# Whole weights in place of two halves for the products beside attention's queries

## The chip, the cores and the metric

The kernel runs on one core of a Trainium2 chip. The metric is the device time of one execution in microseconds (us). TensorE multiplies (PE in the profile; PEld are its weight loads), VectorE (DVE), ScalarE (ACT) and GpSimd (POOL) work on elements, SyncE (SP) issues nearly all transfers.

## The reference

Attention without a softmax, a norm over each head, and a feed-forward block behind it. The feed-forward weights arrive as 64-bit floats.

```python
kv = np.einsum('bhsd,bhse->bhde', k, v)          # 8 batches, 8 heads, 576 tokens, 64 wide
out = np.einsum('bhsd,bhde->bhse', q, kv)
rms = np.sqrt(np.mean(out * out, axis=-1, keepdims=True) + 1e-06)
x = (out / rms * g_norm)                         # -> (4608, 512)
h = x @ w_in                                     # (512, 2048)
r = np.maximum(h, 0.0)
return ((r * r) @ w_out)                         # (2048, 512)
```

## The kernel before

**Tiling.** The 4608 tokens are nine strips of 512 (`N_STRIP`), and each strip is four tiles of 128 tokens. The feed-forward block of a strip has an up part (x times w_in, squared ReLU) and a down part (times w_out). Both use Strassen's scheme: a block product is computed as seven smaller ones of sums and differences of the blocks, in the order of `ORDER` or `DEEP_ORDER`. In strip 0 the up part is plain (`up_first`, L898), and its down part has one level. Strip 1 has one level in the up part (`up`) and two in the down part (`down_deep`). From strip 2 on (`DEEP_UP`) both parts have two levels: seven products of seven small products each.

**Small products.** A small product of the up part is `up_small`: four 128 by 128 products, each with 128 rows of contraction, 128 columns of weights and 128 columns of moving activations. In the down part it is `small_products`: four products that add up in one 128 by 128 place of PSUM. Both call `halved_product` for each of the four. It issues two matmuls with 64 columns of weights each, the second writing the other 64 partitions of PSUM (L852). The one-level products go through `product` (L857), with 128 columns of weights and 256 of moving data. Everything is in 32-bit floats.

**Attention.** It runs beside the feed-forward work, a strip or more ahead, as a list of small steps, `slices`. The ones that use PE late in the kernel are `key_value` (L435: k times v, 128 rows by 64 columns of weights, then the rest of the tokens with 64 rows by 64 columns) and `products_x` (L471: the queries times kv, 64 rows by 64 columns, 64 matmuls for a pair of tiles, 32 for a single one). The step `query` calls `key_value` first if it was given keys, then `products_x`, then squares on ACT. The further steps (means, roots, scaling, a transpose, sending x to DRAM) are on DVE, ACT and SP.

**What sets the order.** The program order of each engine is that in which Python issues: there is no scheduler behind it. From strip 2 on the loop at the end of the kernel has 55 slots for the up part (`up_slot`) and 14 steps for the down part. After each slot, `attend_between` looks at the next slices and issues them when its estimates of the backlog of DVE and ACT allow it (`ON_DVE`, `ON_ACT`, `BEHIND`). So a run of queries comes at the end of a slot, between the small products of two slots. The planner's estimates do not depend on how a small product is issued. In strip 1, slices are spread evenly over the first 25 steps by `attend`.

**Tiles that products wait for.** PSUM has five buffers for products (`ps_A`, `ps_B`, `ps_C` take turns) and one each for x_ps (two banks) and other uses. A buffer comes free when ACT or DVE has read it (`snap`, L1315, is such a copy).

Of the kernel before, what the change touches and what calls it, by code (L numbers as in the profile page):

```python
# [20 lines left out]
def kernel(  # L21
# [34 lines left out]
    nc = tc.nc  # L56
# [17 lines left out]
    DEEP_UP = 2  # L74
# [216 lines left out]
    def minus(eng, out, a, b):  # L291
        eng.tensor_tensor(out=out, in0=a, in1=b, op=ALU.subtract)  # L292
# [125 lines left out]
    def key_value(b, *ps_of):  # L418
        while any(f == load and a[:2] == (b, p) or f == load_rest and a[0] == b for _, f, a in keys_due for p in ps_of):
            _, f, a = keys_due.popleft()  # L420
            f(*a)
        ps = apsum.tile([P, len(ps_of), D], FP32, name="kv_ps", tag="at")
        if (b, ps_of[0]) == (0, 0):
            keep_busy(ps[:, 0], 3)
            warm = apsum.tile([P, NT, P], FP32, name="x_ps", tag="first")[:, 0]
        half = slice(REST * (b % 2), REST * (b % 2 + 1))
        tiles = [[main.pop((n, b, p)) for n in "kv"] for p in ps_of]
        steps = [(i, c) for i in range(len(ps_of)) for c in range(C)] + [(i, C) for i in range(len(ps_of))]
        for i, c in steps:
            if (b, ps_of[i], c) == (0, 0, C):  # L430
                keep_busy(warm, 2)
            for h in range(2):
                at = (slice(None), h, c) if c < C else (half, 2 * ps_of[i] + h)
                a, w = (t[at] for t in (tiles[i] if c < C else (k_rest, v_rest)))
                nc.tensor.matmul(  # L435
                    ps[ts(h, D), i], lhsT=a, rhs=w, start=i == 0 and c == 0, stop=c == C, skip_group_check=True
                )
        at = (NP * b + ps_of[0]) % (2 * NP)
        d = kv_all[:, at : at + len(ps_of)]
        nc.scalar.copy(d[0:D, :, 0:D], ps[0:D])  # L440
        nc.scalar.copy(d[D:P, :, D:P], ps[D:P])
        for i, p in enumerate(ps_of):
            kvd[b, p] = d[:, i]
            if b < 2:
                if b == 1 and p == 0:
                    load_next()
            else:
                u = next(to_load, None)
                if u is not None:
                    keys_later(load, *u, nc.sync, "kv")  # L450
                if p == (1 if b > 3 else NP - 1) and b + 1 < B:
                    keys_later(load_rest, b + 1, nc.sync)
# [3 lines left out]
    def products_x(ns):  # L456

        ps = apsum.tile([P, 2, 2, d_model // 2], FP32, name="x_ps", tag="x", bufs=1)
        for p in range(NP):
            for i, n in enumerate(ns):  # L460
                m, c = divmod(n, PAIR)
                for h in range(2):
                    half = slice(REST * h, REST * (h + 1))
                    if c == C:
                        q, b = qT["rest", m, p], 2 * m + h
                    else:
                        b, c_b = (2 * m, c) if c < C else (2 * m + 1, c - C - 1)
                        q = qT[b, p][:, c_b]
                    for r in range(2):
                        row = slice(D * r, D * (r + 1))  # L470
                        nc.tensor.matmul(  # L471
                            ps[half, r, i, ts(p, D)], lhsT=q[row, half], rhs=kvd[b, p][row, row], start=True, stop=True
                        )
        return ps

    def squared_parts(parts, pool=xn_pool, tag="x_n"):
        sqs = []
        for ps in parts:
            sqs.append(pool.tile(list(ps.shape), FP32, name="sq", tag=tag))
            nc.scalar.activation(sqs[-1], ps, AF.Square)  # L480
        return sqs
# [26 lines left out]
    def query(ns, *keys):  # L508
        if keys:
            key_value(*keys)  # L510
        ps = products_x(ns)
        parts = [ps[:, :, i] for i in range(len(ns))]
        queried.append((parts, squared_parts(parts, c_pool, "c")))

    def query_means(ns):
        ps = products_x(ns)
        parts = [ps[:, :, i] for i in range(len(ns))]
        queried.append((parts, mean_of(squared_parts(parts))))
# [171 lines left out]
    slices, ready = [], {}  # L690
# [30 lines left out]
    for b in range(2, B):  # L721
        pairs = query_pairs(b)
        for i, pair in enumerate(pairs):
# [8 lines left out]
            if more and b > 2 and left == 1 + b % 2:  # L732
                slices.append((T, (b + 1, 0)))
            slices.append((query, (pair, *keys)))
            if b == 2:
                slices += [(T, (3, 1))] * (left == 1) + [(mean_roots, (pair,)), (normalized, (pair,))]
# [20 lines left out]
    slice_at = [0]  # L757
# [84 lines left out]
    def open_bank(p):  # L842
# [2 lines left out]
            bank[b] = fpsum.tile([P, 2, 2 * P], FP32, name=f"ps_{b}", tag="f")  # L845
        return bank[b]

    def halved_product(ps, lhsT, rhs, start, stop):

        for h in range(2):  # L850
            half = slice(P // 2 * h, P // 2 * (h + 1))
            nc.tensor.matmul(ps[half], lhsT=lhsT[:, half], rhs=rhs, start=start, stop=stop, skip_group_check=True)  # L852
# [21 lines left out]
    def quarters(s, g):  # L874

        if (s, 11) not in gq:
            for q in (11, 12, 21, 22):
                gq[s, q] = g_pool.tile([P, FQ, TH], FP32, name="gt", tag="gt")
        return {q: gq[s, q][:, 2 * g : 2 * g + 2, :] for q in (11, 12, 21, 22)}
# [6 lines left out]
    def sum_g3(s, g):  # L886
        dest = quarters(s, g)
        minus(nc.vector, dest[12], dest[11], dest[12])
# [182 lines left out]
    def small_products(s, p, js):  # L1071
        c = "B" if p in (4, 2, 5, 3) else "A"
        if js[0] == 1 and p not in (6, 7, 3):
            opened[c] = set()
            n = 2 + (s == N_STRIP - 1 and p == 5)
            chain[c] = [fpsum.tile([P, 4, P], FP32, name=f"ps_{c}", tag="f") for _ in range(n)]
            if n == 3:
                chain[c].append(apsum.tile([P, 2, 4, P], FP32, name="ps_x", tag="x", bufs=1)[:, 0])
                chain[c].append(apsum.tile([P, 4, P], FP32, name="ps_at", tag="at"))
        for j in js:  # L1080
            x, i = place(s, p)[j]
            a, w = leaf[p][j], w_blk.pop((s, p, j))
            for f in range(FQ // 2):
                halved_product(
                    chain[c][x][:, i, :], a[:, f, :], w[:, f, :], x not in opened[c] and f == 0, f == FQ // 2 - 1
                )
            opened[c].add(x)
# [199 lines left out]
    def up_small(s, n, p, j, slot):  # L1287
# [6 lines left out]
        for i in range(4):  # L1294
            if j in (5, 6, 3):
                w = w_blk["in", s, p][:, (5, 6, 3).index(j), ts(i, P)]
            else:
                kc, f = {1: (0, 0), 2: (1, 0), 4: (1, 1), 7: (0, 1)}[j]
                w = w_half(b, kc, f)[:, i // 2, ts(i % 2, P)]
            halved_product(ps[:, i, :], w, rhs, j in (1, 2, 5) and i == 0, True)  # L1300
# [47 lines left out]
    for s in range(N_STRIP):  # L1348
# [13 lines left out]
        n_up = len(steps)  # L1362
# [5 lines left out]
        goal, begun = ready.get(s + 1, len(slices)), slice_at[0]  # L1368
        if s >= DEEP_UP:
            goal = max(goal, min(ready[DEEP_UP] + (len(slices) - ready[DEEP_UP]) * (s - 1) // (N_STRIP - DEEP_UP - 1), len(slices)))  # L1370
            if s > DEEP_UP:
                goal = min(pair_ends, key=lambda end: abs(end - goal))
        total, done = sum(w for w, _, _ in steps), 0
        for i, (w, fn, a) in enumerate(steps):
# [25 lines left out]
            if s == 0 and n_up + 2 <= i < n_up + 4:  # L1400
                for g in range(2 * (i - n_up) - 4, 2 * (i - n_up) - 2):
                    sum_g3(0, g)
            fn(*a)
            if s == 0 and i < 4:

# [91 lines left out]
```

## Time and profile before

| what | value |
|---|---|
| median of three runs | 874.2 us |
| the three runs | 869.32, 874.2, 876.95 us |
| time of the profiled execution | 869.32 us |
| its span, first to last instruction | 867.5 us |
| granted TensorE clock | 1.0 over the whole span |
| matmuls | 14176, and as many weight loads |
| halved matmuls in strips 1 to 8 (L852) | first at 195.5 us, mean of one 273 ns |
| weight load of a half / of a whole L857 product | 137 / 190 ns |
| runs of query products (L471) behind 195.5 us | 13, from 244.3 to 706.3 us |
| runs of key-value products (L435) behind 195.5 us | 9 |

How to read it: a matmul's duration reaches from the start of its pass to the last result in PSUM, and several are under way at a time. What one costs in a stream is therefore the distance from its start to the next one's, which the timeline gives as the start of a group and the number of matmuls in it, and the single records give one by one. In the timeline each line is a group of like instructions: start, time from the first one's start to the last one's end, engine, line, operation, result<-operands, rows*columns of the weights, shape of the moving data, count. The page names the waits that the profile infers from semaphores. A stretch in which PE is between two shapes of matmul has no such row.

### The profile page before, as it was taken

Reading aid. Unit: us, or ns where it says so; the run is one execution under the profiler, and the core shown is the slowest. Engines: PE = TensorE matmul, PEld = TensorE weight load, DVE = VectorE, ACT = ScalarE, POOL = GpSimd, SP = SyncE. Lnnn points to the kernel's source line nnn. Section 1 sums busy time; section 2 is a strip of 40 time slices with the busy share of each in tenths; the row PEclk is TensorE's granted clock in tenths of the full one; section 3 lists DMA queues with packets and bytes.
Section 4 is the critical chain, followed back from the end, with each engine's and each line's share of the span. In section 5 each row is a group of like instructions: output and inputs, shape, how many; then the busy total and the mean of one; then the engine's idle time right before and its main releaser. Section 6 shows DMA issues by size and latency. Waiting matters only on the chain.

```text
span 867.5 us, 32585 instructions
## 1 busy us (share of the span) xinstructions
PE 860.8 (99%) x14176; PEld 805.7 (93%) x14176; DVE 720.3 (83%) x1236; ACT 352.2 (41%) x805; POOL 315.2 (36%) x319
## 2 busy tenths in 40 slices
PE   9999999999999999999999999999999999999998
PEld 7445888889999999999999999999999999999998
DVE  3999998879877996789689977897889777976887
ACT  5799251320048403750356034901491148102810
POOL 1100004630459323730574045704470447145700
PEclk9999999999999999999999999999999999999999
DMA  9998997999999997989688979997668856875483
GB/s 317 302 339 251 279 376 229 285 325 374 290 256 262 343 319 230 238 311 335 211 244 272 341 240 265 287 311 268 210 223 301 303 168 215 294 283 195 173 313 126
DMA packets 169470, 236.47 MB, mean 273 GB/s; under 512 B 78704, under 2 KB 133744, under 8 KB 161008
## 3 DMA queue, kind: packets, MB, share of 16 engines
q1 hardware_dynamic: 169024, 234.33, 83.5%
q8 instruction: 111, 1.82, 0.9%
q14 instruction: 31, 0.25, 0.1%
q10 hardware_dynamic: 304, 0.07, 0.0%
HBM read 197.66 MB, written 36.70 MB: 270 GB/s over the span
## 4 chain that ended last, share of the span: by engine, by line
PE 83%; DVE 9%; ACT 3%; DMA 3%; issue 2%; SPq 0%; DVEq 0%; ACTq 0%
PE ps_A L852 36%; PE ps_B L852 32%; PE ps_C L852 5%; PE ps_A L857 4%; PE kv_ps L435 2%; DVE w_c L272 2%; PE x_ps L471 2%; PE ps_B L857 2%; DVE w_t L292 1%; DMA w_deep<-w_t 1%; DVE wt L292 1%; DMA first_qkv<-in_v_dram 1%; DVE w_c L266 1%; PE ps_C L857 1%; DVE w_in L275 1%
## 5 line engine op out<-in xcount | busy, mean ns | idle before, releaser
L852 PE MATMUL ps_B<-w_blk,g_s 128*64 128x128 f32 x2016 | 121.8, 273 | 0.0
L852 PEld LDWEIGHTS ps_B<-w_blk,g_s 128*64 128x64 f32 x2016 | 112.4, 137 | 0.1
L852 PE MATMUL ps_A<-x_l,w_in 128*64 128x128 f32 x1568 | 102.8, 273 | 0.7 <-ACT snap L1315 0.6
L292 POOL TENSOR_TENSOR x_l<-xT 128x256 f32<-128x256 f32 x21 | 16.1, 765 | 228.6 <-PE ps_A L852 228.6
L852 PE MATMUL ps_B<-w_blk,gt 128*64 128x128 f32 x1504 | 93.9, 273 | 0.0
L852 PE MATMUL ps_A<-w_blk,g_s 128*64 128x128 f32 x1536 | 92.0, 273 | 0.0
L852 PEld LDWEIGHTS ps_A<-x_l,w_in 128*64 128x64 f32 x1568 | 89.0, 137 | 0.9 <-ACT snap L1315 0.8
L1310 POOL TENSOR_TENSOR snap<-snap,gt 128x512 f32<-128x512 f32 x35 | 46.3, 1322 | 113.4 <-ACT snap L1315 104.1
L852 PEld LDWEIGHTS ps_A<-w_blk,g_s 128*64 128x64 f32 x1536 | 85.5, 137 | 0.0
L852 PEld LDWEIGHTS ps_B<-w_blk,gt 128*64 128x64 f32 x1504 | 84.4, 137 | 0.3 <-issue 0.3
L1315 ACT COPY snap<-ps_A 128x512 f32<-128x512 f32 x63 | 36.9, 585 | 103.6 <-PE ps_A L852 94.4
L1250 ACT ACTIVATE gt<-gt 128x512 f32<-128x512 f32 x112 | 70.1, 626 | 8.8 <-DVE gt L1310 8.8
L1251 ACT ACTIVATE gt<-gt 128x512 f32<-128x512 f32 x112 | 70.7, 631 | 3.6
L852 PE MATMUL ps_A<-w_blk,gt 128*64 128x128 f32 x1152 | 71.0, 273 | 0.0
L1099 ACT COPY o_sb<-ps_A 128x128 f32<-128x128 f32 x24 | 6.4, 266 | 144.9 <-PE ps_A L852 115.4
L852 PEld LDWEIGHTS ps_A<-w_blk,gt 128*64 128x64 f32 x1152 | 64.5, 137 | 0.0
L292 DVE TENSOR_TENSOR gt<-gt 128x2048 f32<-128x2048 f32 (+1 forms) x29 | 59.7, 2063 | 0.0
L1098 DVE TENSOR_TENSOR o_sb<-o_sb,ps_B 128x256 f32<-128x256 f32 (+1 forms) x123 | 47.5, 386 | 14.5 <-ACT o_sb L1099 9.4
L1310 POOL TENSOR_TENSOR gt<-gt,snap 128x512 f32<-128x512 f32 x42 | 52.6, 1282 | 14.9 <-DVE snap L1310 14.9
L852 PE MATMUL ps_B<-x_l,w_blk 128*64 128x128 f32 x784 | 51.4, 273 | 0.0
L852 PE MATMUL ps_A<-x_l,w_blk 128*64 128x128 f32 x784 | 51.2, 273 | 0.0
L1099 ACT COPY o_sb<-ps_B 128x128 f32<-128x128 f32 x31 | 8.2, 266 | 96.3 <-PE ps_B L852 96.3
(194 smaller groups left out, 1838.1 us busy)
## 6 DMA issues: line engine op xcount, KB each, us to landing
w_blk<-w_deep SPq DMA_DIRECT2D x56, 1024.0 KB, 7.2
w_blk<-w_out SPq DMA_DIRECT2D x56, 768.0 KB, 6.5
w_blk<-w_in_deep SPq DMA_DIRECT2D x49, 768.0 KB, 6.0
raw<-in_moe_w_in_dram SPq DMA_DIRECT2D x16, 512.0 KB, 7.8
raw<-in_moe_w_out_dram SPq DMA_DIRECT2D x16, 512.0 KB, 5.2
k<-in_k_dram SPq DMA_DIRECT2D x29, 256.0 KB, 5.1
v<-in_v_dram SPq DMA_DIRECT2D x29, 256.0 KB, 5.3
x_d<-x_q SPq DMA_DIRECT2D x27, 256.0 KB, 4.9
```

Source lines behind the costliest of these rows:

```text
L272: yield nc.vector.scalar_tensor_tensor(out=ci, in0=high, scalar=-(2**30), in1=ci, op0=ALU.bitwise_and, op1=ALU.bitwise_or)
L292: eng.tensor_tensor(out=out, in0=a, in1=b, op=ALU.subtract)
L435: nc.tensor.matmul(ps[ts(h, D), i], lhsT=a, rhs=w, start=i == 0 and c == 0, stop=c == C, skip_group_check=True)
L471: nc.tensor.matmul(ps[half, r, i, ts(p, D)], lhsT=q[row, half], rhs=kvd[b, p][row, row], start=True, stop=True)
L852: nc.tensor.matmul(ps[half], lhsT=lhsT[:, half], rhs=rhs, start=start, stop=stop, skip_group_check=True)
L857: nc.tensor.matmul(bank[BANK[p]][:, i, :], lhsT=lhsT(k), rhs=rhs(k), start=p in (1, 5, 2) and i == 0 and k == 0, stop=k == n - 1, skip_gro ...
L1098: add = lambda out, a, b: nc.vector.tensor_tensor(out=out, in0=a, in1=b, op=ALU.add)
L1099: yield nc.scalar.copy(q[:, 3:4], small(1))
L1250: nc.scalar.activation(o, o, AF.Relu)
L1251: nc.scalar.activation(o, o, AF.Square)
L1310: add = lambda eng, out, a, b: eng.tensor_tensor(out=out, in0=a, in1=b, op=ALU.add)
L1315: nc.scalar.copy(t, ps)
```

## The change

A counter, `whole`, is added. While it is positive, `halved_product` issues one matmul with all 128 columns of weights and counts down; at zero it issues two halves as before. `query` sets the counter to 12 when its products are issued, which is three small products. The loop sets it to at least 4, one small product, ahead of a step of the up part from strip 2 on, when the next slice is a query. Where the planner holds a query back for some slots, that happens at each of them.

```diff
@@ query
         parts = [ps[:, :, i] for i in range(len(ns))]
         queried.append((parts, squared_parts(parts, c_pool, "c")))
+        whole[0] = BEHIND_QUERY
@@ halved_product
+    AHEAD, BEHIND_QUERY = 4, 12
+    whole = [0]
+
     def halved_product(ps, lhsT, rhs, start, stop):

+        if whole[0]:
+            whole[0] -= 1
+            nc.tensor.matmul(ps, lhsT=lhsT, rhs=rhs, start=start, stop=stop, skip_group_check=True)
+            return
         for h in range(2):
             half = slice(P // 2 * h, P // 2 * (h + 1))
             nc.tensor.matmul(ps[half], lhsT=lhsT[:, half], rhs=rhs, start=start, stop=stop, skip_group_check=True)
@@ the loop over the steps of a strip
+            if DEEP_UP <= s and i < n_up and slice_at[0] < goal and slices[slice_at[0]][0] == query:
+                whole[0] = max(whole[0], AHEAD)
             fn(*a)
```

As built, this gives 264 whole products: 12 at the start of the down part of strip 1, where the last queries of strip 1's up part had set the counter, 12 behind each of 13 runs of queries, and 96 in groups of 4 to 16 in front of 12 of these runs.

## The prediction

> **What bounds the kernel now.** I read the page's busy shares first, then the chain that ended last, then the waits of PE, and last the timeline of PE around one visit of attention's queries. The page:
>
> ```profile
> PE 860.8 (99%) x14176; PEld 805.7 (93%) x14176; DVE 720.3 (83%) x1236; ACT 352.2 (41%) x805; POOL 315.2 (36%) x319
> ...
> PE 83%; DVE 9%; ACT 3%; DMA 3%; issue 2%; SPq 0%; DVEq 0%; ACTq 0%
> PE ps_A L852 36%; PE ps_B L852 32%; PE ps_C L852 5%; PE ps_A L857 4%; PE kv_ps L435 2%; DVE w_c L272 2%; PE x_ps L471 2%; PE ps_B L857 2%; DVE w_t L292 1%; DMA w_deep<-w_t 1%; DVE wt L292 1%; DMA first_qkv<-in_v_dram 1%; DVE w_c L266 1%; PE ps_C L857 1%; DVE w_in L275 1%
> ```
>
> PE is busy 99% of the span, and the halved products (L852) alone are 73% of the chain. The DVE and DMA shares of the chain lie before 195 us, ahead of every edit. The waits of PE from 190 us to the end are two short rows:
>
> ```profile
> PE ps_A L852 <- ACT snap L1315: 0.6, 1, 0.6
> PE x_ps L471 <- issue: 0.2, 1, 0.2
> ```
>
> So behind 195 us the end is the sum of PE's start-to-start times, and whatever is added between two matmuls there is added to the kernel. I therefore work in start-to-start times, not in durations: a half lasts 273 ns, but 112 of them take 6.11 us in the chain, that is 109.1 ns per pair of halves.
>
> **What a change of shape costs.** PE runs three shapes here: halves (128 rows by 64 columns of weights, L852; the key-value products L435 have the same shape), the queries' 64 by 64 (L471), and whole ones (128 by 128). One visit of queries between halves, timeline of PE (start, us from first start to last end, then the group):
>
> ```profile
> 438.71 1.04 PE L852 MATMUL ps_A<-x_l,w_in 128*64 128x128 f32 x16
> 439.69 0.34 PE L471 MATMUL x_ps<-kv_all,qT_rest 64*64 64x64 f32 x8
> 439.85 0.30 PE L471 MATMUL x_ps<-kv_all,qT 64*64 64x64 f32 x8
> 439.97 0.30 PE L471 MATMUL x_ps<-kv_all,qT_rest 64*64 64x64 f32 x8
> ...
> 440.55 0.30 PE L471 MATMUL x_ps<-kv_all,qT 64*64 64x64 f32 x8
> 440.78 1.09 PE L852 MATMUL ps_C<-x_t,w_in 128*64 128x128 f32 x16
> 441.70 0.50 PE L852 MATMUL ps_B<-x_t,w_blk 128*64 128x128 f32 x6
> ```
>
> Sixteen halves take 0.873 us in a steady run. Before the queries they take 0.98: leaving halves costs 0.10. Behind the queries they take 0.92: entering halves costs 0.05 (the single records say 160 ns from the first pair to the second, against 109). Entering the queries costs 0.05 too (0.16 to the second group, against 0.117), and leaving them 0.11; both stay. A change of shape is thus about 0.15 us in which PE multiplies nothing.
>
> The whole shape at 128 columns of moving data stands in the opening, where first_queries (L585) comes behind halves, and where transposes (L611) go over to halves (L407):
>
> ```profile
> 9.22 1.09 PE L407 MATMUL t_ps<-ident,q 128*64 128x128 f32 x16
> 10.24 1.16 PE L585 MATMUL x_ps<-kv_all,qT 128*128 128x128 f32 x8
> 11.33 0.69 PE L435 MATMUL kv_ps<-v,k 128*64 128x64 f32 x16
> ```
>
> ```profile
> 15.20 0.66 PE L611 MATMUL xt_ps<-ident,x_n 128*128 128x128 f32 x4
> 15.78 1.09 PE L407 MATMUL t_ps<-ident,first_qkv 128*64 128x128 f32 x16
> ```
>
> The sixteen halves of L407 take 1.02 us: 0.873, plus 0.05 for entering and 0.10 for leaving. The eight whole ones of L585 start 213 ns apart once and then 112, 112, 111 (single records): a steady whole product costs 111.7 ns, and entering whole costs 0.102. That a first load of 128 columns isn't hidden shows also in L857, whose first matmul behind the queries at 109.43 us is followed after 320 ns, the others after 216. Leaving whole for L435 or L407 costs 0.093 (205 against 112; 203 against 109), and 0.05 for entering the halves.
>
> So the steady rates hardly differ, 111.7 against 109.1, and **the price is in the changes of shape**. For this last point a rule of the Trainium skill says otherwise: by "TensorE: Matmul & The Clock Gate", Part 3 (Packing small matmuls), a weight load runs beside matmuls in flight only where the row group differs. L585 uses all rows in each product and still starts every 112 ns, so this trace disagrees; by that rule each whole product would take the 213 ns of an unhidden load and the change would cost 27 us.
>
> **The change part by part.** The order of instructions of the two built programs is the same on every engine but PE, DMA queues included; no wait is added and nothing is moved past anything. On PE 264 pairs of halves become 264 whole products, from 195 us on. What follows from where they stand:
>
> 1. The first 12 follow the last L857 products, which are whole already. Before: whole to halves; after: the same change 12 products later. Nothing.
> 2. Thirteen visits of queries have 12 whole products behind. Entering whole in place of halves: 13 x (0.102 - 0.051) = 0.66 us.
> 3. Behind these 12 there is a change from whole to halves that did not exist: 13 x (0.093 + 0.051) = 1.87 us.
> 4. Eleven of the visits get a group of 4 to 16 whole ones in front, behind halves: 11 x (0.100 + 0.102) = 2.22 us. Of the other two, one gets none (the call of the planner takes the slice of means and the query in one step), and one has 8 between keys and queries, where it enters whole in place of halves: 0.05 us.
> 5. In seven of the eleven, key-value products stand between the group and the queries. They have the shape of halves, and before there was no change (L852 to L435 goes on at the steady distance, 102 to 103 ns from a second half to the next first). After: 7 x (0.093 + 0.049) = 0.99 us. In the other four the whole group is left for the queries in place of halves: 0.093 against 0.100, nothing.
> 6. 264 x (111.7 - 109.1) ns = 0.69 us.
>
> The sum is 0.66 + 1.87 + 2.22 + 0.05 + 0.99 + 0.69 = **6.5 us**, all on PE and all behind 195 us, so nothing hides it. What can be taken off: one stall of PE in the records, at 551.43 us, 0.76 us over the steady distance (the first row of PE's waits gives 0.6 of it to ACT's snap), lies 15 us behind a visit. A later PE waits less there. How much cannot be read, since most of the delay in front of the queries delays ACT's work on them as much; only the 0.2 us behind the queries is a true head start for ACT. I take 0.1 and keep 0 and 0.76 as ends. In the other direction, a group delayed by some tenths of a microsecond could find ACT or POOL in a new place; the largest such stall in the trace is that same 0.76, so I allow one of them.
>
> Against the profiled execution (869.3 us, span 867.5): 869.3 + 6.4 = 875.7. The three runs before spread from 869.32 to 876.95 around the median 874.2, so the profiled one is the fastest of them; on the median the forecast is **880.6 us**, slower by 0.7%. The ends of the costs: 6 could be nothing (109.1 for the whole too, as the transposes of L611 have it), and the stall gone whole: 6.5 - 0.69 - 0.76 = 5.0. Upward: 6.5 + 0.76 = 7.3. So 879.2 to 881.5 from the terms, to which the spread of the runs adds some 3 us on both sides.
>
> **Rivals.**
>
> *The whole shape needs no emptying of PE.* If PE pulled the load of a whole product ahead across the border, terms 2 to 5 would vanish, and the way out of the queries (0.11 + 0.05) with them: 0.69 - 13 x 0.16 - 0.76 = -2.2 us, 872.0, no slower than before. It decides at the first matmul behind the queries. For it: only that L641 and L857, both whole, follow each other with no loss. Against it: L857 behind L471 at 109.43 us starts 0.148 behind the last query product, just as L852 does, and then loses 0.104 more. I find no way to a gain over 1%; that would need 8.7 us, and all thirteen visits with everything lost around them (0.10 + 0.05 + 0.11 + 0.05 each) hold 4.0.
>
> *Whole products run at the unhidden load.* If operands of the small products (strided parts of the activations, weights just fetched) kept the load from running ahead, each would cost up to 213 ns as the first of L585 does: 264 x (213 - 109) = 27.5 us in place of term 6, with 5.8 of the changes: 33 us, 907, slower by 3.8%. Any mean above 121 ns for the whole ones would carry the sum past 1%. For it: no whole product at this size with these operands is in the trace. Against it: L585 at 112, and L857 at 216 for twice the columns, with weights from gt and w_blk.
>
> *The stalls multiply.* Each visit puts 0.4 to 0.55 us into PE's order; the planner spaces ACT's work behind queries by its own costs. If each visit met one new stall like that at 551 us: 13 x 0.76 = 9.9 us on top, 890. Against it: a later PE gives the engines that feed it time, it doesn't take any.
>
> **How the numbers follow.** Forecast, slower by 5.0 to 7.3 us: 0.84. Free changes of shape: 0.06. Unhidden loads or stalls: 0.10. With a median of runs that spread by 7.6 us, a measurement tells about 1% from no change, and the forecast lies just inside: from 880.6 to the bound at 882.9 are 2.3 us, which the spread of a median (some 3 us, an estimate from the range of the three runs) and of the terms goes past about one time in five. So slower by over 1%: 0.84 x 0.21 + 0.10 = 0.28. Faster by over 1%: 0.02, from the spread in the first rival. Within 1%: 0.70. The range is 875 to 887: the terms with the spread of medians on both sides, with a little toward the stalls, and leaves out the ends of the rivals.
>
> **What the changed profile should show.** Whole products at 128 x 128 in groups of 4 to 16, 264 in all and 264 matmuls fewer; the first of each group lasting some 0.10 longer than the next ones, these at 275 ns and 112 apart; 0.148 us from the last query product's start to the first whole and 0.213 more to the second; a gap of 0.205 between the last whole and the first half; visits with keys longer by 0.54 and without by 0.39, plus 2.6 ns for each whole product; and the stretches between the visits unchanged at 6.11 us for 112 halves. I am wrong if the whole ones stand more than 121 ns apart, if they start at once behind the queries, or if PE shows new waits between the visits.

## The result

The changed kernel takes 878.2 us, the median of 13 runs (875.2 to 881.3), against 871.5 for the kernel before (13 runs, 869.2 to 877.0). The ratio is 1.0069, with a 95% interval from 1.0048 to 1.0089: slower by 6.0 us (4.2 to 7.8). That is also the difference of the means, 878.1 and 872.1; the two medians differ by 6.7. The 874.2 us that the prediction started from was a high median of three. A second set gave the same ratio, 1.0069 (1.0047 to 1.0091).

TensorE is as full as before and has more to do. The page of the changed kernel, with its busy shares and its chain (L856 are the whole products, L860 the halves, L865 the one-level products; the lines have moved by eight):

```profile
PE 867.6 (99%) x13648; PEld 808.1 (92%) x13648; DVE 720.1 (82%) x1236; ACT 352.3 (40%) x805; POOL 313.9 (36%) x319
...
PE 81%; DVE 9%; DMA 4%; issue 2%; ACT 2%; POOL 1%; SPq 1%; DVEq 0%; POOLq 0%
```

The busy time of PE went from 860.8 to 867.6 with 528 matmul records fewer, and the other engines moved by at most 1.3 us. The count matters: 264 whole products in place of 528 halves should be 264 matmuls fewer. **The trace has two records for each 32-bit matmul of the program.** A small product of four matmuls shows as eight whole records or sixteen halves.

One visit of queries without keys, timeline of PE (start, us from first start to last end, engine, group):

```profile
439.74 1.04 PE L860 MATMUL ps_A<-x_l,w_blk 128*64 128x128 f32 x16
440.72 1.16 PE L856 MATMUL ps_A<-x_l,w_in 128*128 128x128 f32 x8
441.71 1.06 PE L856 MATMUL ps_B<-x_l,w_blk 128*128 128x128 f32 x8
442.60 1.06 PE L856 MATMUL ps_A<-x_t,w_in 128*128 128x128 f32 x8
443.50 1.06 PE L856 MATMUL ps_A<-x_l,w_in 128*128 128x128 f32 x8
444.48 0.34 PE L471 MATMUL x_ps<-kv_all,qT_rest 64*64 64x64 f32 x8
...
445.58 1.16 PE L856 MATMUL ps_C<-x_t,w_in 128*128 128x128 f32 x8
446.57 1.06 PE L856 MATMUL ps_B<-x_t,w_blk 128*128 128x128 f32 x8
447.46 1.06 PE L856 MATMUL ps_A<-x_l,w_blk 128*128 128x128 f32 x8
448.45 1.09 PE L860 MATMUL ps_A<-x_l,w_in 128*64 128x128 f32 x16
449.38 0.49 PE L860 MATMUL ps_B<-x_l,w_blk 128*64 128x128 f32 x5
```

A whole small product in the middle of a group takes 0.89 us (441.71 to 442.60), a halved one 0.873. The first of a group takes 0.99 (440.72 to 441.71), 0.10 more. The halves ahead of the group take 0.98, so they lose 0.10 too. The last whole small product takes 0.99, since the first half stands 205 ns behind its last record (447.46 to 448.45), and the halves that follow take 0.93. In single records the visit has exactly the distances of the prediction: 203 ns from the last half to the first whole, then 213 and 112; 148 or 149 from the last query product to the first whole; 205 from the last whole to the first half, and 160 to the second pair.

That the first load of weights is in the open can be read from the row of the loads. In the group behind the queries, a load starts 0.11 us ahead of its product (446.46 against 446.57); the first load of the group starts only with its product (445.57 against 445.58):

```profile
445.57 0.97 PEld L856 LDWEIGHTS ps_C<-x_t,w_in 128*128 128x128 f32 x8
446.46 0.97 PEld L856 LDWEIGHTS ps_B<-x_t,w_blk 128*128 128x128 f32 x8
```

With keys, the border from whole to keys is new as well:

```profile
330.03 1.04 PE L860 MATMUL ps_B<-w_blk,g_s 128*64 128x128 f32 x16
331.01 1.16 PE L856 MATMUL ps_C<-xT,w_in 128*128 128x128 f32 x8
332.10 1.15 PE L435 MATMUL kv_ps<-v,k 128*64 128x64 f32 x32
333.18 0.38 PE L435 MATMUL kv_ps<-v_rest,k_rest 64*64 64x64 f32 x5
```

The eight whole records here take 1.09 us up to the keys, where a steady run would give 0.89: 0.10 at the way in and 0.09 at the way out. The same visit in the kernel before:

```profile
328.95 1.04 PE L852 MATMUL ps_C<-xT,w_in 128*64 128x128 f32 x16
329.82 1.10 PE L435 MATMUL kv_ps<-v,k 128*64 128x64 f32 x32
330.85 0.38 PE L435 MATMUL kv_ps<-v_rest,k_rest 64*64 64x64 f32 x5
```

There the halves went over to the keys at their steady distance (0.87 us for sixteen), and the keys took 1.03 us. In the changed kernel they take 1.08 (332.10 to 333.18).

The waits of PE have no row for these borders, but those of the weight loads have some, in the second profile of the changed kernel eleven of 0.17 us ahead of L856, one for each of the eleven borders from halves to whole of term 4. Ten are put to issue and one to DVE. The profile lists a wait from 0.15 us on, so the 0.12 us by which the loads stand still at a border out of whole have no row.

To compare kernels without the accidents of one execution I add up PE's row of single records: from the start of the last one-level product (at about 195 us) to the start of the last matmul, less each distance inside a run of one shape by as much as it exceeds the steady one (the first loads of a run stay in, and less a wait of 1.2 us between keys and queries in the second profile of the kernel before). The kernel before gives 667.6 to 668.0 us in four profiles, the changed one 674.7 to 675.0 in four. The difference of 7.0 us is what the order and the shapes cost by themselves, and the runs below are measured by it too.

### The profile page after: what moved, and what is told of

Read it like the earlier page. It is cut to its first block, busy times and chain, and to the rows that moved or that the text cites. A ratio compares the mean times of both kernels' runs of the same rounds, so it can differ in the third digit from the quotient of the medians.

```text
span 876.4 us, 31529 instructions
## 1 busy us (share of the span) xinstructions
PE 867.6 (99%) x13648; PEld 808.1 (92%) x13648; DVE 720.1 (82%) x1236; ACT 352.3 (40%) x805; POOL 313.9 (36%) x319
## 4 chain that ended last, share of the span: by engine, by line
PE 81%; DVE 9%; DMA 4%; issue 2%; ACT 2%; POOL 1%; SPq 1%; DVEq 0%; POOLq 0%
PE ps_A L860 32%; PE ps_B L860 27%; PE ps_A L865 4%; PE ps_C L860 3%; PE ps_A L856 3%; PE ps_B L856 3%; DVE w_c L272 2%; PE kv_ps L435 2%; PE x_ps L471 2%; PE ps_B L865 2%; DVE w_t L292 1%; PE ps_C L856 1%; DMA w_deep<-w_t 1%; DVE wt L292 1%; DVE w_in L275 1%
## 5 line engine op out<-in xcount | busy, mean ns | idle before, releaser
L860 PE MATMUL ps_B<-w_blk,g_s 128*64 128x128 f32 x1840 | 110.7, 273 | 0.0
L860 PEld LDWEIGHTS ps_B<-w_blk,g_s 128*64 128x64 f32 x1840 | 102.4, 137 | 0.5
L860 PE MATMUL ps_B<-w_blk,gt 128*64 128x128 f32 x1472 | 92.2, 273 | 0.8 <-DMA w_blk<-w_deep 0.8
L860 PE MATMUL ps_A<-w_blk,g_s 128*64 128x128 f32 x1536 | 92.2, 273 | 0.0
L860 PE MATMUL ps_A<-x_l,w_in 128*64 128x128 f32 x1376 | 90.0, 273 | 0.6 <-ACT snap L1323 0.4
L860 PEld LDWEIGHTS ps_A<-w_blk,g_s 128*64 128x64 f32 x1536 | 85.7, 137 | 0.0
L860 PEld LDWEIGHTS ps_B<-w_blk,gt 128*64 128x64 f32 x1472 | 82.8, 137 | 1.1 <-PE ps_B L860 1.0
L860 PEld LDWEIGHTS ps_A<-x_l,w_in 128*64 128x64 f32 x1376 | 77.9, 137 | 1.4 <-ACT snap L1323 0.7
L860 PE MATMUL ps_A<-w_blk,gt 128*64 128x128 f32 x1152 | 71.2, 273 | 0.0
L860 PEld LDWEIGHTS ps_A<-w_blk,gt 128*64 128x64 f32 x1152 | 64.7, 137 | 0.0
L1106 DVE TENSOR_TENSOR o_sb<-o_sb,ps_B 128x256 f32<-128x256 f32 (+1 forms) x123 | 47.5, 386 | 15.2 <-ACT o_sb L1107 10.1
L1318 DVE TENSOR_TENSOR gt<-ps_A,gt 128x512 f32<-128x512 f32 x49 | 32.8, 682 | 16.5 <-PE ps_A L860 14.9
L1064 DVE TENSOR_TENSOR g_s<-gt 128x512 f32<-128x512 f32 x56 | 46.3, 827 | 0.0
```

The lines of the kernel that those rows point to most:

```text
L1064: nc.vector.tensor_tensor(out=t, in0=a21, in1=a22, op=ALU.add)
L1106: add = lambda out, a, b: nc.vector.tensor_tensor(out=out, in0=a, in1=b, op=ALU.add)
L1318: add = lambda eng, out, a, b: eng.tensor_tensor(out=out, in0=a, in1=b, op=ALU.add)
```

## The experiments

**Single whole products everywhere, and the same number in groups.** Both start from the kernel before and take no account of where the queries stand. The first makes one of 32 products whole (calls of `halved_product`, not small products of four).

```diff
+    halved_calls = [0]
+
     def halved_product(ps, lhsT, rhs, start, stop):
+        halved_calls[0] += 1
+        if halved_calls[0] % 32 < 1:          # the other kernel: % 128 < 4
+            nc.tensor.matmul(ps, lhsT=lhsT, rhs=rhs, start=start, stop=stop, skip_group_check=True)
+            return
         for h in range(2):
```

> Before, with every 32nd small product of the halved kind issued whole, wherever it falls: 91 whole ones in 91 groups. My theory, that the price is in the changes of shape (0.202 us from halves to whole, 0.144 back), expects 91 x 0.346 + 91 x 0.005 = 31.9 us more than before, some 3.7%. The rival that the price lies in the whole products themselves (6.0 us measured / 264 = 23 ns each) expects 91 x 0.023 = 2.1 us. The rival that it is their place beside the queries, where ACT and DVE are late, expects about nothing, since most of these stand elsewhere.

Measured: ratio 1.0352 (1.0324 to 1.0379), 30.6 us (28 to 33). PE's row is 31.8 us longer. One of the 91 groups in its timeline:

```profile
401.24 1.70 PE L858 MATMUL ps_B<-w_blk,g_s 128*64 128x128 f32 x28
402.87 0.49 PE L854 MATMUL ps_B<-w_blk,g_s 128*128 128x128 f32 x2
403.29 1.09 PE L858 MATMUL ps_B<-w_blk,g_s 128*64 128x128 f32 x16
404.21 1.92 PE L858 MATMUL ps_A<-w_blk,gt 128*64 128x128 f32 x32
```

One whole product (two records) holds PE from 402.87 to 403.29, 0.42 us, with 0.10 lost before it (28 halves take 1.53 in a steady run, here 1.63) and 0.05 behind it (0.92 for sixteen). A pair of halves would have done it in 0.218.

> Before, with 4 consecutive ones of every 128 halved products issued whole: the same 91 whole products, but in 23 groups. Changes of shape: 22 x 0.346 + 0.5 = 8.1 us more than before (0.9%), a quarter of the run with single ones. Price in the whole products: 2.1 us, the same as with single ones. Place beside the queries: about nothing.

Measured: ratio 1.0088 (1.0067 to 1.0109), 7.7 us, and 8.5 on PE's row. The same 91 whole products cost a quarter with a quarter of the groups. So the whole product is not what costs, and nor is its place; the number of changes of shape is.

**No halves at all.** `halved_product` issues one matmul, always.

```diff
     def halved_product(ps, lhsT, rhs, start, stop):
+        nc.tensor.matmul(ps, lhsT=lhsT, rhs=rhs, start=start, stop=stop, skip_group_check=True)
+        return
         for h in range(2):
             half = slice(P // 2 * h, P // 2 * (h + 1))
```

> Before, with all 2940 halved products issued whole, so that changes are left only where queries and keys stand. In the trace each 32-bit product shows as two matmul records, 111.7 ns apart for whole and 109.1 for a pair of halves, so the steady price is 5.1 ns a product. Changes of shape: 2940 x 5.1 ns = 15.0 us, and 13 x 0.051 behind queries, 9 x 0.142 into keys, less the one border that goes: 16.8 us more than before in all (1.9%). Price of 23 ns in each whole product: 68 us. Unhidden loads (213 for each record): some 600 us.

Measured: ratio 1.0175 (1.0157 to 1.0194), 15.2 us (13.7 to 16.9); PE's row is 16.3 us longer. Steady small products in it, with operands of the up part:

```profile
438.35 1.06 PE L850 MATMUL ps_B<-x_l,w_blk 128*128 128x128 f32 x8
439.24 1.06 PE L850 MATMUL ps_A<-x_t,w_in 128*128 128x128 f32 x8
440.14 1.06 PE L850 MATMUL ps_A<-x_l,w_in 128*128 128x128 f32 x8
441.03 1.06 PE L850 MATMUL ps_C<-x_t,w_in 128*128 128x128 f32 x8
```

Eight records take 0.893 us (438.35 to 441.03 for three groups), 111.7 ns each, against 109.1 for a pair of halves. Loads stay hidden for all of the kernel's operands, and the steady price is 2.6 ns a record, 5.1 ns a product. It is small, and over 2940 products it is more than the change itself costs.

**Longer groups, the same number of them.**

```diff
-    AHEAD, BEHIND_QUERY = 4, 12
+    AHEAD, BEHIND_QUERY = 4, 24
```

> The changed kernel with 24 whole products behind each run of queries in place of 12 (432 whole ones in all, 4 to 16 in front as before): the same number of groups. Changes of shape: 5.8 + 432 x 0.0051 = 8.0 us more than before, 0.9 more than the changed kernel. Price in the whole products: 432 x 0.023 = 9.9 us. Place beside the queries: as the changed kernel, 6 us.

Measured: ratio 1.0082 (1.0059 to 1.0106), 7.1 us, and 7.9 on PE's row, 0.9 more than the changed kernel's 7.0. The times alone cannot tell 7.1 from 6.0; PE's row agrees with the steady price and not with 23 ns a product, which would have given 3.9 more.

**Each part alone.**

```diff
-    AHEAD, BEHIND_QUERY = 4, 12
+    AHEAD, BEHIND_QUERY = 0, 12           # the other kernel: 4, 0
```

> The changed kernel with the groups in front of the queries left as halves: 168 whole products, 12 behind each of 13 runs of queries and 12 at the start. Changes of shape: 13 x (0.051 + 0.144) + 168 x 0.0051 = 3.4 us more than before (0.39%). If the place behind the queries were the cause, nearly all of the 6 us; if the place in front, nothing.

Measured: ratio 1.0028 (1.0010 to 1.0046), 2.4 us (0.9 to 4.0); PE's row 3.2 us longer.

> The changed kernel with the 12 behind each run of queries left as halves: 96 whole products in 12 groups in front. Changes of shape: 11 x 0.202 + 7 x 0.142 for the border to the keys + 0.05 + 96 x 0.0051 = 3.7 us more than before (0.43%), though it has fewer whole products than the run with those behind alone. Price in the whole products: 96 x 0.023 = 2.2 us, less than that run's 3.9.

Measured: ratio 1.0031 (1.0011 to 1.0052), 2.7 us (1.0 to 4.5); PE's row 3.8 us longer. Both parts cost, and by their borders. The one in front has fewer whole products and costs at least as much on PE's row, because seven of its twelve groups stand ahead of keys and bring two new borders each, halves to whole and whole to keys, where the others bring one. On PE's row the parts add up, 3.2 + 3.8 = 7.0.

**More profiles of both kernels.** No edit.

> The changed kernel once more, for a second profile. If the stalls of TensorE at 240, 291, 382 and 558 us in its first profile belong to the change, they come back at these places with their sizes; if they belong to the execution (transfers landing late), their places and sizes differ, and what stays is 7.1 us of borders and steady price.

> The kernel before once more, for a second profile: the borders and the 109.1 ns for a pair of halves come back as they were; the stalls at 245, 250 and 551 us (1.35 us in all) may move.

Waits of PE from 196 us on, first and second profile of the changed kernel:

```profile
PE ps_B L860 <- DMA w_blk<-w_deep: 0.8, 1, 0.8
PE ps_A L860 <- POOL x_t L292: 0.6, 1, 0.6
PE ps_A L860 <- ACT snap L1323: 0.4, 1, 0.4
PE ps_A L860 <- DVE gt L1318: 0.2, 1, 0.2
```

```profile
PE ps_A L860 <- ACT snap L1323: 0.4, 1, 0.4
PE ps_A L860 <- DVE gt L1318: 0.2, 1, 0.2
```

Two stalls come back, at 290 us (DVE) and 556 us (ACT); the two largest, on a transfer at 382 us and on POOL at 240 us, are in none of the other three profiles of this kernel. Whether the change has no part in them is not shown: a wait on the same transfer, w_blk from w_deep, of 0.2 to 0.6 us stands in three of the kernels above (groups in front alone, 24 behind, and 4 of 128) and in none of the four profiles of the kernel before. The kernel before, second profile:

```profile
PE x_ps L471 <- issue: 2.5, 2, 1.4
PE ps_A L852 <- ACT snap L1315: 0.6, 1, 0.6
PE ps_A L852 <- DVE gt L1310: 0.2, 1, 0.2
```

It has the same two regular stalls (the first profile of the kernel before has only the one on ACT), and 2.5 us in which the queries' products waited for nothing that the profile shows.

> The kernel before, a third profile. The runs so far came out about 1 us below their borders and steady prices. If that is because the kernel before stalls more, at the queries' products above all (waits of TensorE on L471 that the profile puts to issue, 0.2 us in its first profile and 2.5 us in its second), they come again here, 0.2 to 2.6 us. If they are chance of one execution, they may be absent.

> The changed kernel, a third profile. If whole products around the queries keep these waits away, there is none on L471 again, as in its first two profiles. If they are chance, some of 0.2 to 1.5 us may be there.

> The kernel before, a fourth profile, for the same question as the third: waits of TensorE on L471 put to issue again (0.2 to 2.6 us), or none.

> The changed kernel, a fourth profile, for the same question as its third: no wait of TensorE on L471 put to issue, or some of 0.2 to 1.5 us.

In the third profiles both kernels have the two regular stalls alone, and PE's stretch from 195 us to the last matmul is 668.96 us before and 675.79 after, 6.8 more. The fourth profile of the kernel before has two irregular waits again, the changed kernel's none of that size:

```profile
PE ps_A L852 <- issue: 0.9, 1, 0.9
PE ps_A L852 <- ACT snap L1315: 0.6, 1, 0.6
PE ps_A L852 <- DVE gt L1310: 0.2, 1, 0.2
PE x_ps L471 <- issue: 0.2, 1, 0.2
```

Irregular stalls, as sums over the single records: 0.6, 3.1, 0.0 and 1.5 us before; 1.8, 0.0, 0.0 and 0.1 after. Waits put to issue on the query products stand in three of four profiles before and in none of four after, though the single records of the fourth have 0.1 us there. They come back with the part behind the queries alone, where the groups in front are missing (0.4 us), and not with the groups in front alone. That fits an instruction supply that fewer matmuls in front of the queries relieve. But four profiles with such spread do not show it, and no run varied the supply by itself. It stays open whether the 0.8 us by which these means differ belongs to the change.

## Why the prediction was right

The forecast was 6.4 us more than before; it came out at 6.0 (4.2 to 7.8), within 1%. The mechanism held at every border, and one term of the sum was mis-sized. That 6.4 lies so near to 6.0 is in part luck: with that term and the stall below put right the sum is 7.0, still inside the interval but further off. And the forecast time of 880.6 us stood on a median that was 2.7 us high; 878.2 was measured.

*Term 1*, the first 12 products: the first whole record stands 215 ns behind the last one-level product, whose steady distance is 216, and the halves 205 behind the last whole. Nothing was added, as said.

*Terms 2 to 5*, the changes of shape: 0.051, 0.144, 0.202 and 0.142 us were taken from the opening and from the visits, where the same shapes follow each other with other operands. The changed kernel has each of them at the same size to a few ns. The runs with single and grouped whole products confirm the price of a group as a whole, 31.8 us on PE's row for 91 groups against 31.9 expected.

*Term 6*, the steady price, was wrong by a factor of two. It counted 264 whole products at 2.6 ns; the rows that gave 2.6 ns are records, and a product has two. So it is 264 x 5.1 ns = 1.35 us in place of 0.69, and the sum 7.1 in place of 6.5. PE's row gives 7.0. The same slip made "264 matmuls fewer" of 528, and put the visits 2.6 ns a product too short: from the single records, the same work at the same place became 0.53 us longer in the visit at 440 us, of which 0.39 is borders, and 0.62 in the one at 330 us, of which 0.54 is. The rival of unhidden loads was priced with the same slip: 528 records at 213 in place of 109 ns would have been some 55 us and not 27.5, and the bound of 121 ns for a gap some 115. The counts were there to be compared beforehand: a small product is four matmuls in two halves each, and the timeline showed it as sixteen records.

*The stall at 551 us* shrank from 0.76 to 0.60 us (at 556 in the second profile), by 0.16 where 0.1 was taken. The rest between 7.0 on PE's row and 6.0 in the times is within the interval; the irregular stalls above are a candidate for it, and no more.

*The rivals.* That the whole shape needs no emptying of PE falls with the 148 and 213 ns behind the queries. Unhidden loads fall with 111.7 ns over a whole kernel. Here the Trainium skill's page "TensorE: Matmul & The Clock Gate", Part 3 (Packing small matmuls), has loads run beside matmuls only where the row group differs. Products that all use every row ran at 111.7 ns with only the first of a group at 213, so the measurement decides against that "only" for this form. The same section also lets a load go ahead into a background weight buffer, which the prediction left out; these distances do not speak against that. Multiplying stalls did not come: the regular one on ACT is in all four profiles of both kernels and shrank, and the one on DVE, in three of four before and in all four after, grew by no more than 0.05 us where it was.

The chances had the time within 1% of before, with slower next; 0.7% is inside that bound, and 13 runs of each kernel were enough to tell it from none.

## What to carry to other kernels

On an engine that is busy throughout, count the changes of array shape and not only the products: here each group of whole products between halves cost 0.35 us, as much as three pairs of half records take, whatever the length of the group. Read the price of a border from start-to-start distances at a place in the trace where the same two shapes meet, since the multiplying engine's waits have no row for it and those of the loads name only some, with a releaser that explains nothing. And before multiplying a distance by a count from the program, check how many records one instruction of the program leaves.

## What the runs showed of the hardware

Leaving a shape costs 0.09 to 0.10 us behind halves and whole products, and 0.11 behind the 64 by 64 query products. Entering one costs what of the first load of weights is in the open: 0.05 us for 64 columns (loads of 137 ns) and 0.10 for 128 (190 ns). The columns alone do not set it: the transposes of L611 in the kernel before, 128 columns too but with loads of 140 ns, lose 0.06 (166 ns once, then 109).

The Trainium skill's page "TensorEngine Tiling (Array Packing)", section Key Properties, says that changing the tiling mode drains TensorE, without a figure. This case agrees as far as a trace can: the price stands at each change of shape and not between two lines of one shape (halves to keys, before), and 91 groups put it at 0.35 us in and out. The emptying itself has no row.

That two halves run steadily faster than one whole product of the same size, 109.1 ns a pair of records against 111.7 ns a record, was known from the opening; that this holds for all operands of the kernel was not, and all 2940 products whole, with their borders to queries and keys, cost 15.2 us (13.7 to 16.9). Why it is 2.6 ns was not tested.
